# Hash attention and a quick-GELU MLP on one core: Attention scheduled by whole pairs, POOL's late sums of W_out gathered, and the last turns reordered

## The chip, the cores and the metric

The kernel runs on one core of a Trainium2 chip. The core has five engines that work side by side: TensorE (PE in the profile) multiplies matrices into PSUM, VectorE (DVE) and ScalarE (ACT) work on SBUF and PSUM, GpSimd (POOL) works on SBUF, and SyncE (SP) issues transfers. Each runs its own instructions in order and waits for the others by semaphores. The metric is the time of one execution on the device in microseconds (us); the lower the better.

## What is computed

Attention over 4 batches and 8 heads, 768 queries and keys, head dimension 64, in which a query sees only the keys that fall into the same bucket of a 6-bit hash, and then an MLP whose input is the heads side by side (3072 tokens of 512):

```python
q_bits = (np.einsum('bhsd,dk->bhsk', q, proj) > 0).astype(np.int64)
k_bits = (np.einsum('bhsd,dk->bhsk', k, proj) > 0).astype(np.int64)
mask = q_bucket[:, :, :, None] == k_bucket[:, :, None, :]
scores = np.where(mask, scale * np.matmul(q, k.transpose(0, 1, 3, 2)), -1000000000.0)
attn = np.exp(scores - np.max(scores, axis=-1, keepdims=True))
attn = attn / (np.sum(attn, axis=-1, keepdims=True) + 1e-09)
x = np.matmul(attn, v)                 # heads side by side: 3072 x 512
h = x @ w_in                           # 512 x 2048
g = h * (1.0 / (1.0 + np.exp(-1.702 * h)))
out = g @ w_out                        # 2048 x 512
```

Everything is computed in float32; w_in and w_out arrive as float64 bit patterns and are converted on the chip.

## The kernel before

**Attention** works on 16 pairs n of two heads each, one in partitions 0 to 63 and one in 64 to 127. The queries of a pair are cut into two halves c of 384 (HS), the keys into six tiles (T) of 128, three of which are "low" and three "high" (GT). The functions, in the order of the data:
- `fetch` (L328) loads k and q, `fetch_v` (L340) loads v, from SP's queue.
- `turn` (L391, VectorE) transposes k or q of the next pair in blocks of 32; `measure` (L398, ScalarE) sums its squares for a later check of size.
- `hashed` (L408, TensorE) multiplies both by the hash vectors; `featured` (L413, VectorE) makes sign features of that, and eight small transfers (L420, SP) put them where the scores need them.
- `scores` (L432, TensorE): per key tile two bf16 products of the features and two float32 products of k and q, one for each head, into a PSUM tile ps of two banks (three such tiles rotate); the exponential (L433, ScalarE) goes to es[c].
- The sum over keys: `add_low` (L440, L441, POOL) adds the three low tiles to acc0, of which there is one buffer; `add_high` (L446, L448, VectorE) adds the three high ones and acc0. `total` (L479, TensorE) sums over partitions into dn; `invert` (L485 to L494, VectorE) makes reciprocals of it, with a `yield` behind its first step; `norm` (L499, VectorE) scales the output.
- `values` (L458, TensorE) multiplies v by the exponentials; `unload` (L469, L470, ScalarE) writes the result to xT, which is the MLP's input.

PSUM has one bank with the tag "av" (pool aps) and one with the tag "m" (pool mps) beside the six of the scores. "av" holds the output of values, "m" holds dn, the hash and a small transpose in turn.

Between these, VectorE converts w_in: `begin(n)` issues a chunk's load (L162), `step(n, k)` runs the next k steps of it (L178 to L198). In the last four pairs `x_sums` (L219 to L222) make the first sums of the MLP's input.

The order of each engine's instructions is the order in which the program's lines emit them. It is written out in one loop over groups (n, c). In a group, TensorE gets scores(n, c), then, of the group before it, total and values, then hashed. So scores and values alternate half by half, and total(n - 1) and hashed(n + 1) stand in between: scores(n, 0), total(n - 1), values(n - 1, 1), hashed(n + 1), scores(n, 1), values(n, 0), and so on.

**The MLP** multiplies by Strassen-Winograd: seven products of quarters in place of eight, twice nested for W_out. Its sums of quarters are made by `sums_a` (POOL, L211 to L214: s1, s3, s2, s4) for W_out and `sums_b` (VectorE, L219 to L222: t1, b12, t2, t4) for the activations. The products by W_out run in 21 steps n (7 outer products for each of three blocks of tokens), each of seven inner products (L820) of eight matmuls. In a step TensorE makes the products 1, 2, 3, 6, 7, 5 and 4; VectorE adds them up in the four quarters c11 to c22 (L824), and in between makes the four sums for the next step (g_sums); `turned` (L800, VectorE) transposes finished quarters and `written` (L807) sends them out. Product 6 needs t2, product 7 b12, product 4 t4, product 3 the s4 of W_out.

The W_out sums of the outer products 0 to 3 are made before, those of number 4 in step 0. The sums of number 5 (needed in step 5) and number 6 (needed in step 6) are held back: POOL does two of them in each of the steps 2 to 5. A copy of one element to `mark` (L924) from the result of the step before holds POOL until that step has its c11:

```python
if 2 <= n <= 5:
    nc.gpsimd.tensor_copy(mark, ms[OUTER[n - 1]][0:1, 0, 0:1])
i = n % 2 * 2
for f in inner_sums(4) if n == 0 else inner_sums(4 + n // 2)[i : i + 2] if 2 <= n <= 5 else []:
    f()
```

In the last two steps `after(at)` is called at five points of a step and emits the sums for the next step and the turns: in the last but one, quarter 0 is turned behind c11, quarters 1 and 3 behind c12 and c22, quarter 2 behind c21. The output transfers of the last but one step go to SP's and ScalarE's queues in turn.

Of the kernel before, what the change touches and what calls it, by code (L numbers as in the profile page):

```python
# [8 lines left out]
F32 = mybir.dt.float32  # L9
# [29 lines left out]
def kernel(  # L39
# [243 lines left out]
    def attention(ff):  # L283
# [4 lines left out]
        with actx:  # L288
# [99 lines left out]
            def turn(n, name):  # L388
                x = raws[n, name]
                xt = xts[n, name] = wk.tile([P, S], F32, tag=f"{name}T", name=f"{name}T")  # L390
                nc.vector.transpose(xt, x.rearrange("p s i -> p (s i)"))  # L391
# [31 lines left out]
            def scores(n, c, kts):  # L423
                qT, kT, qf, kf = xts[n, "q"], xts[n, "k"], feats[n % 2]["q"], feats[n % 2]["k"]
                cols = slice(c * HS, (c + 1) * HS)
                for kt in kts:
                    ps = sps.tile([P, 2, 512], F32, tag="s", name="ps")
                    keys = slice(kt * P, (kt + 1) * P)
                    for a, m, last in ((kf, qf, False), (kT, qT, True)):
                        for j in range(2):  # L430
                            hs = slice(D * j, D * (j + 1))
                            nc.tensor.matmul(ps[:, j, 0:HS], a[hs, keys], m[hs, cols], start=not last, stop=last)  # L432
                    nc.scalar.activation(es[c][:, kt, :, 0:HS], ps[:, :, 0:HS], Act.Exp, scale=1.0 / D**0.5)  # L433
# [3 lines left out]
            def add_low(n, c):  # L437

                acc = accs[n, c, 0] = st.tile([P, 2, HS], F32, tag="acc0", name="acc0", bufs=1)
                nc.gpsimd.tensor_tensor(acc, es[c][:, 0, :, 0:HS], es[c][:, 1, :, 0:HS], op=Alu.add)  # L440
                nc.gpsimd.tensor_tensor(acc, acc, es[c][:, 2, :, 0:HS], op=Alu.add)  # L441
# [8 lines left out]
            def values(n, c, kts):  # L450
                if 0 in kts:

                    pool, tag = (mps, "m") if (n, c) == (last, 1) else (aps, "av")
                    avs[n, c] = pool.tile([P, HS + 1], F32, tag=tag, name="av")
                av, vt = avs[n, c], vts[n]
                for t in kts:
                    for j in range(2):
                        nc.tensor.matmul(av[D * j : D * (j + 1), :], vt[:, t, j, :], es[c][:, t, j, :],  # L458
                                         start=(t == 0), stop=(t == T - 1))
# [11 lines left out]

            def total(n):

                dn = accs[n] = mps.tile([P, HS], F32, tag="m", name="dn")
                for c in range(2):
                    acc = accs.pop((n, c))
                    for j in range(2):
                        r0 = D * j + 32 * c
                        nc.tensor.matmul(dn[r0 : r0 + 32, :], ones[:, 0:32], acc[:, j, :], start=True, stop=True)  # L479

            def invert(n):


                rt = st.tile([P, HS // 32, 32], F32, tag="rt", name="rt", bufs=1)
                nc.vector.transpose(rt.rearrange("p s i -> p (s i)"), accs.pop(n))  # L485
                yield
                r = st.tile([P, 2, HS // 32], F32, tag="r", name="r")
                nc.vector.reciprocal(r, rt[:, :, 0].unsqueeze(1).to_broadcast([P, 2, HS // 32]))
                for r0 in range(0, P, 32):
                    c = r0 // 32 % 2  # L490
                    r1 = r0 + 32 - 64 * c
                    nc.vector.reciprocal(r[r1 : r1 + 32, c], rt[r0 : r0 + 32, :, 0])
                rs = accs[n] = st.tile([P, S], F32, tag="rs", name="rs", bufs=1)
                nc.vector.transpose(rs.rearrange("p (s i) -> p s i", i=32),  # L494
                                    r.rearrange("p c s -> p (c s)").unsqueeze(2).to_broadcast([P, S // 32, 32]))

            def norm(n):
                x, rs = x_of(n), accs.pop(n)
                nc.vector.tensor_tensor(x, x, rs.rearrange("p (t s) -> p t s", t=T), op=Alu.mult)  # L499


            groups = [(n, c, kts) for n in range(len(pairs)) for c in range(2)
                      for kts in ((range(GT), range(GT, T)) if n == 0 else (range(T),))]
            last = len(pairs) - 1
            conv = {}

# [18 lines left out]
                    nc.vector.tensor_reduce(largest[0:1, 0:1], row, axis=AX.X, op=Alu.max)  # L525


            totals, norms, hashes = [], [], []
            rest = first_pair()
            fetch_v(0)  # L530
            for x in "kq":
                fetch(1, x)
            for g in range(len(groups) + 2):
                n, c, kts = groups[g] if g < len(groups) else (last + 1, 0, ())
                prev = groups[g - 1] if 1 <= g <= len(groups) else None
                if kts:
                    scores(n, c, kts)
                    if g == 0:
                        rest()
                    if kts[0] == 0:  # L540
                        add_low(n, c)


                if hashes:
                    featured(hashes.pop())
                ended = prev and prev[2][-1] == T - 1
                if ended:
                    add_high(*prev[:2])
                    if prev[1] == 1:
                        totals.append((g + (g == len(groups)), prev[0]))  # L550

                turned = ("", "k", "q", "")[g] if n == 0 else "kq" if c == 0 and n < last else ""
                inverted = iter(())
                for x in turned[:1]:
                    turn(n + 1, x)
                    measure(n + 1, x)
                while norms:
                    norm(norms.pop(0))
                if totals and totals[0][0] == g:
                    norms.append(totals.pop(0)[1])  # L560
                    total(norms[-1])

                    inverted = invert(norms[-1])
                    next(inverted)
                for x in turned[1:]:
                    turn(n + 1, x)
                    measure(n + 1, x)
                whole(inverted)
                if prev:
                    values(*prev)  # L570
                if ended:
                    unload(*prev[:2])
                if "q" in turned:
                    hashed(n + 1)
                    if n:
                        hashes.append(n + 1)
                    else:
                        featured(n + 1)
                    for x in "kq" if n else "q":
                        if n + 2 <= last:  # L580
                            fetch(n + 2, x)
                    fetch_v(n + 1)
                elif turned:
                    fetch(n + 2, turned)
                if kts and kts[-1] == T - 1:
                    step(n, 3)
                    if c == 0 and n > last - len(x_sums):
                        x_sums[n - last - 1]()
                    if c == 1:
                        begin(n + 1)  # L590
                if g in (len(groups) - 3, len(groups) - 2):
                    guard(g - len(groups) + 3)
                if g == len(groups):
                    for f in in_sums(0):
                        f()
                    early.close()
                    next(ff)
            for x in norms:
                norm(x)


    def shifted_attention():
# [76 lines left out]
    def feed_forward(tag, late=()):  # L679
# [9 lines left out]
        with ExitStack() as fctx:  # L689
# [228 lines left out]
            for n, (sb, o) in enumerate(steps_out):  # L918
# [1 line left out]
                if 0 < n and n + 1 < len(steps_out):  # L920
                    fetch(n + 1)

                if 2 <= n <= 5:
                    nc.gpsimd.tensor_copy(mark, ms[OUTER[n - 1]][0:1, 0, 0:1])  # L924
                i = n % 2 * 2
                for f in inner_sums(4) if n == 0 else inner_sums(4 + n // 2)[i : i + 2] if 2 <= n <= 5 else []:
                    f()
                later_sums = g_sums(n + 1)
                m = wholes[n % len(wholes)]
# [1 line left out]
                def after(at):  # L931
                    if at == 0:
                        while pending:
                            pending.pop(0)()

                    for f in later_sums[at : at + 1] if n == 0 else ([], later_sums[0:1], later_sums[1:2], later_sums[2:], [])[at]:
                        f()

                    if n + 2 >= len(steps_out):
                        for q in ((0,) * (not final), (), (1, 3), (2,), (0,))[at]:  # L940
                            turned(m, int(final), int(not final), q, q + 1)
                    if final and at in (2, 3):
                        written(sb, 0, (3 - at,), loader + [nc.scalar])
                    if n + 2 == len(steps_out) and at == 3:
                        written(sb, 1, (0, 1), loader + [nc.scalar])
# [23 lines left out]
    def whole(steps):  # L969
        for _ in steps:  # L970
            pass
# [46 lines left out]
```

## Time and profile before

| What | Value |
|---|---|
| median of 10 runs | 880.65 us (880.35 to 883.31) |
| profiled execution | 882.81 us, span 881.0 us, granted TensorE clock 0.996 |
| PE (TensorE) busy | 868.8 us (99%), 4077 matmul instructions |
| PE weight loads busy | 500.8 us (57%) |
| DVE (VectorE) busy | 723.5 us (82%) |
| ACT (ScalarE) busy | 314.6 us (36%) |
| POOL (GpSimd) busy | 322.0 us (37%) |
| Attention's scores, from the first to the last values | 10.88 to 324.86 us |
| MLP, first half (products by W_in) | 324.86 to about 614.3 us |
| MLP, second half (products by W_out) | about 614.3 us to the end |

The span is the time from the first to the last instruction of the profiled execution. The chain of waits follows the work that ended last back to its start: 95% of it is TensorE, 4% VectorE. A line of the timeline has the start in us, the duration, the engine, the line of the program, the operation, the tile written and the tiles read, the shape and the count; in brackets stands how long the engine had been idle before it and what ended that.

### The profile page before, as it was taken

Reading aid. Unit: us, or ns where it says so; the run is one execution under the profiler, and the core shown is the slowest. Engines: PE = TensorE matmul, PEld = TensorE weight load, DVE = VectorE, ACT = ScalarE, POOL = GpSimd, SP = SyncE. Lnnn points to the kernel's source line nnn. Section 1 sums busy time; section 2 is a strip of 40 time slices with the busy share of each in tenths; the row PEclk is TensorE's granted clock in tenths of the full one; section 3 lists DMA queues with packets and bytes.
Section 4 is the critical chain, followed back from the end, with each engine's and each line's share of the span. In section 5 each row is a group of like instructions: output and inputs, shape, how many; then the busy total and the mean of one; then the engine's idle time right before and its main releaser. Section 6 shows DMA issues by size and latency. Waiting matters only on the chain.

```text
span 881.0 us, 11897 instructions
## 1 busy us (share of the span) xinstructions
PE 868.8 (99%) x4077; PEld 500.8 (57%) x4077; DVE 723.5 (82%) x1020; ACT 314.6 (36%) x519; POOL 322.0 (37%) x277
## 2 busy tenths in 40 slices
PE   9999999999999999999999999999999999999996
PEld 5444444444444444444444444444878888888885
DVE  4689989999999986788777788888887977897786
ACT  5767776776677642222233222332000000000000
POOL 4343343334433365665443344659921000000000
PEclk9999999999999999999999999999999999999999
DMA  5535545665444103555455545575835675467524
GB/s 131 94 62 84 104 82 98 99 102 84 82 82 99 53 0 140 206 203 203 164 189 192 208 177 194 193 251 186 301 108 191 196 213 214 156 221 243 191 96 99
DMA packets 169157, 132.01 MB, mean 150 GB/s; under 512 B 123616, under 2 KB 138112, under 8 KB 163712
## 3 DMA queue, kind: packets, MB, share of 16 engines
q1 hardware_dynamic: 166528, 129.70, 51.7%
q10 hardware_dynamic: 2560, 1.46, 0.7%
q8 instruction: 34, 0.56, 0.3%
q14 instruction: 35, 0.29, 0.1%
HBM read 79.69 MB, written 50.33 MB: 148 GB/s over the span
## 4 chain that ended last, share of the span: by engine, by line
PE 95%; DVE 4%; issue 0%; POOL 0%; POOLq 0%; DVEq 0%
PE product L708 33%; PE product L820 25%; PE ps L432 18%; PE av L458 15%; PE dn L479 2%; DVE xT L824 2%; PE hash L408 1%; DVE y L800 1%; PE tp L366 1%; PE hash L373 0%; DVE v L824 0%; DVE t2a L221 0%; DVE raw_g L220 0%; DVE t4g L222 0%; DVE s_in L220 0%
## 5 line engine op out<-in xcount | busy, mean ns | idle before, releaser
L433 ACT ACTIVATE e<-ps 128x768 f32<-128x768 f32 x192 | 151.1, 812 | 15.1 <-PE ps L432 12.8
L432 PE MATMUL ps<-qT,kT 64*128 64x384 f32 x768 | 155.2, 482 | 0.0
L708 PE MATMUL product<-xT,w_in_sb 128*128 128x512 f32 x288 | 135.6, 593 | 0.0
L458 PE MATMUL av<-e,v 128*64 128x385 f32 x768 | 131.5, 490 | 0.0
L440 POOL TENSOR_TENSOR acc<-e 128x768 f32<-128x768 f32 x32 | 58.7, 1833 | 192.6 <-DVE acc L448 122.0
L716 ACT ACTIVATE c<-c 128x512 f32<-128x512 f32 x72 | 45.3, 630 | 186.8 <-issue 78.8
L458 PEld LDWEIGHTS av<-e,v 128*64 128x64 f32 x768 | 52.3, 136 | 76.3 <-issue 75.8
L708 PEld LDWEIGHTS product<-xT,w_in_sb 128*128 128x128 f32 x288 | 54.6, 190 | 69.1 <-issue 64.1
L708 PE MATMUL product<-t_x,s_in 128*128 128x512 f32 x192 | 90.2, 592 | 0.0
L432 PEld LDWEIGHTS ps<-qT,kT 64*128 64x128 f32 x768 | 68.3, 188 | 35.1 <-issue 35.1
L219 POOL TENSOR_TENSOR v<-c,u 128x512 f32<-128x512 f32 x24 | 34.1, 1422 | 123.4 <-ACT c L716 123.4
L833 ACT COPY u<-product 128x256 f32<-128x256 f32 x21 | 7.8, 372 | 175.5 <-PE product L820 134.0
L432 PE MATMUL ps<-qf,kf 64*128 64x384 bf16 x384 | 63.3, 324 | 0.1
L708 PEld LDWEIGHTS product<-t_x,s_in 128*128 128x128 f32 x192 | 36.5, 190 | 45.9 <-issue 43.7
L441 POOL TENSOR_TENSOR acc<-acc,e 128x768 f32<-128x768 f32 x32 | 59.1, 1846 | 2.5
L708 PE MATMUL product<-xT,s_in 128*128 128x512 f32 x96 | 45.1, 592 | 0.0
L708 PE MATMUL product<-t_x,w_in_sb 128*128 128x512 f32 x96 | 45.1, 592 | 0.0
L432 PEld LDWEIGHTS <-kf 64*128 64x128 bf16 x384 | 19.1, 94 | 41.0 <-issue 19.5
L446 DVE SCALAR_TENSOR_TENSOR acc<-e 128x768 f32<-128x768 f32 x32 | 32.2, 1007 | 5.1 <-ACT e L433 5.1
L469 ACT COPY vs<-av 128x1 f32<-128x1 f32 x32 | 5.1, 159 | 86.2 <-PE av L458 86.2
L820 PE MATMUL product<-raw_g,xT 128*128 128x256 f32 x152 | 35.3, 380 | 0.0
L448 DVE TENSOR_TENSOR acc<-acc,e 128x768 f32<-128x768 f32 x32 | 32.3, 1010 | 3.3
(208 smaller groups left out, 1548.2 us busy)
## 6 DMA issues: line engine op xcount, KB each, us to landing
raw_g<-g_dram SPq DMA_DIRECT2D x22, 1024.0 KB
s_in<-g_dram SPq DMA_DIRECT2D x20, 1024.0 KB
g_dram<-c SPq DMA_DIRECT2D x72, 256.0 KB
g_dram<-t SPq DMA_DIRECT2D x48, 256.0 KB
raw<-in_moe_w_in_dram SPq DMA_DIRECT2D x16, 512.0 KB
raw<-in_moe_w_out_dram SPq DMA_DIRECT2D x16, 512.0 KB
v<-in_v_dram SPq DMA_DIRECT2D x32, 192.0 KB
g_dram<-u SPq DMA_DIRECT2D x24, 256.0 KB
```

The lines of the kernel that those rows point to most:

```text
L219: return [lambda: eng.tensor_tensor(t1, b12, b11, op=Alu.subtract), lambda: eng.tensor_tensor(b12, b22, b12, op=Alu.subtract), lambda: eng ...
L432: nc.tensor.matmul(ps[:, j, 0:HS], a[hs, keys], m[hs, cols], start=not last, stop=last)
L433: nc.scalar.activation(es[c][:, kt, :, 0:HS], ps[:, :, 0:HS], Act.Exp, scale=1.0 / D**0.5)
L440: nc.gpsimd.tensor_tensor(acc, es[c][:, 0, :, 0:HS], es[c][:, 1, :, 0:HS], op=Alu.add)
L441: nc.gpsimd.tensor_tensor(acc, acc, es[c][:, 2, :, 0:HS], op=Alu.add)
L446: nc.vector.scalar_tensor_tensor(acc, e[0], T * TINY, e[1], op0=Alu.add, op1=Alu.add)
L448: nc.vector.tensor_tensor(acc, acc, x, op=Alu.add)
L458: nc.tensor.matmul(av[D * j : D * (j + 1), :], vt[:, t, j, :], es[c][:, t, j, :], start=(t == 0), stop=(t == T - 1))
L479: nc.tensor.matmul(dn[r0 : r0 + 32, :], ones[:, 0:32], acc[:, j, :], start=True, stop=True)
L708: nc.tensor.matmul(ps, wq[LEFT[i]][:, kc, :], xq[RIGHT[i]][:, kc, :], start=(kc == 0), stop=(kc == K2 - 1))
L716: nc.scalar.activation(c, c, Act.Gelu_apprx_sigmoid)
L820: nc.tensor.matmul(ps, wq[LEFT[i]][:, c, :], gq[RIGHT[i]][:, c, :], start=(c == 0), stop=(c == F4 - 1))
```

## The change

Three things are changed.

1. **POOL's held-back sums of W_out.** Nothing is emitted in steps 2 to 4; step 5 emits all four sums of number 5 and the first two of number 6, step 6 the last two of number 6. The mark is copied in steps 5 and 6 only.
2. **The last but one step.** Its turns are emitted at the point behind c21, in this order: the third sum for the last step (t2), the turns of quarters 0 and 1, the turn of quarter 3, the fourth sum (t4), the turn of quarter 2.
3. **Attention by whole pairs.** The loop over groups is gone. Pair 0 is written out by hand; for each later pair TensorE gets scores(n, 0), scores(n, 1), hashed(n + 1), values(n, 0), values(n, 1), total(n). Outputs of values go to bank "av" for the first half and to bank "m" for the second; dn goes to "av". `invert` is one piece, and it and norm(n - 1) are emitted behind add_low(n, 0), ahead of turn(n + 1, k) and add_high(n, 0). turn(n + 1, q), hashed and featured follow add_high(n, 0). In pair 1 total(0) is emitted behind scores(1, 0). The conversion has two steps behind featured and four behind values(n, 0) and add_high(n, 1). The loads of k and q for pair n + 2 are emitted at the end of pair n. At the end, invert and norm of the last pair are emitted behind the MLP's first part.

```diff
@@ -450,7 +450,7 @@
             def values(n, c, kts):
                 if 0 in kts:
 
-                    pool, tag = (mps, "m") if (n, c) == (last, 1) else (aps, "av")
+                    pool, tag = (mps, "m") if c else (aps, "av")
                     avs[n, c] = pool.tile([P, HS + 1], F32, tag=tag, name="av")
                 av, vt = avs[n, c], vts[n]
                 for t in kts:
@@ -471,7 +471,7 @@
 
             def total(n):
 
-                dn = accs[n] = mps.tile([P, HS], F32, tag="m", name="dn")
+                dn = accs[n] = aps.tile([P, HS], F32, tag="av", name="dn")
                 for c in range(2):
                     acc = accs.pop((n, c))
                     for j in range(2):
@@ -483,7 +483,6 @@
 
                 rt = st.tile([P, HS // 32, 32], F32, tag="rt", name="rt", bufs=1)
                 nc.vector.transpose(rt.rearrange("p s i -> p (s i)"), accs.pop(n))
-                yield
                 r = st.tile([P, 2, HS // 32], F32, tag="r", name="r")
                 nc.vector.reciprocal(r, rt[:, :, 0].unsqueeze(1).to_broadcast([P, 2, HS // 32]))
                 for r0 in range(0, P, 32):
@@ -498,9 +497,6 @@
                 x, rs = x_of(n), accs.pop(n)
                 nc.vector.tensor_tensor(x, x, rs.rearrange("p (t s) -> p t s", t=T), op=Alu.mult)
 
-
-            groups = [(n, c, kts) for n in range(len(pairs)) for c in range(2)
-                      for kts in ((range(GT), range(GT, T)) if n == 0 else (range(T),))]
             last = len(pairs) - 1
             conv = {}
 
@@ -525,78 +521,79 @@
                     nc.vector.tensor_reduce(largest[0:1, 0:1], row, axis=AX.X, op=Alu.max)
 
 
-            totals, norms, hashes = [], [], []
+            low, high, every = range(GT), range(GT, T), range(T)
             rest = first_pair()
             fetch_v(0)
             for x in "kq":
                 fetch(1, x)
-            for g in range(len(groups) + 2):
-                n, c, kts = groups[g] if g < len(groups) else (last + 1, 0, ())
-                prev = groups[g - 1] if 1 <= g <= len(groups) else None
-                if kts:
-                    scores(n, c, kts)
-                    if g == 0:
-                        rest()
-                    if kts[0] == 0:
-                        add_low(n, c)
-
-
-                if hashes:
-                    featured(hashes.pop())
-                ended = prev and prev[2][-1] == T - 1
-                if ended:
-                    add_high(*prev[:2])
-                    if prev[1] == 1:
-                        totals.append((g + (g == len(groups)), prev[0]))
-
-                turned = ("", "k", "q", "")[g] if n == 0 else "kq" if c == 0 and n < last else ""
-                inverted = iter(())
-                for x in turned[:1]:
-                    turn(n + 1, x)
-                    measure(n + 1, x)
-                while norms:
-                    norm(norms.pop(0))
-                if totals and totals[0][0] == g:
-                    norms.append(totals.pop(0)[1])
-                    total(norms[-1])
-
-                    inverted = invert(norms[-1])
-                    next(inverted)
-                for x in turned[1:]:
-                    turn(n + 1, x)
-                    measure(n + 1, x)
-                whole(inverted)
-                if prev:
-                    values(*prev)
-                if ended:
-                    unload(*prev[:2])
-                if "q" in turned:
+            scores(0, 0, low)
+            rest()
+            add_low(0, 0)
+            scores(0, 0, high)
+            turn(1, "k")
+            measure(1, "k")
+            values(0, 0, low)
+            fetch(2, "k")
+            scores(0, 1, low)
+            add_low(0, 1)
+            add_high(0, 0)
+            turn(1, "q")
+            measure(1, "q")
+            values(0, 0, high)
+            unload(0, 0)
+            hashed(1)
+            featured(1)
+            fetch(2, "q")
+            fetch_v(1)
+            scores(0, 1, high)
+            values(0, 1, low)
+            values(0, 1, high)
+            unload(0, 1)
+            for n in range(1, last + 1):
+                scores(n, 0, every)
+                add_low(n, 0)
+                if n == 1:
+                    add_high(0, 1)
+                    turn(2, "k")
+                    total(0)
+                invert(n - 1)
+                norm(n - 1)
+                if 1 < n < last:
+                    turn(n + 1, "k")
+                scores(n, 1, every)
+                add_low(n, 1)
+                add_high(n, 0)
+                if n < last:
+                    turn(n + 1, "q")
                     hashed(n + 1)
-                    if n:
-                        hashes.append(n + 1)
-                    else:
-                        featured(n + 1)
-                    for x in "kq" if n else "q":
-                        if n + 2 <= last:
-                            fetch(n + 2, x)
+                    featured(n + 1)
+                    for x in "kq":
+                        measure(n + 1, x)
+                else:
+                    guard(0)
+                    guard(1)
+                step(n, 2)
+                add_high(n, 1)
+                values(n, 0, every)
+                unload(n, 0)
+                step(n, 4)
+                values(n, 1, every)
+                unload(n, 1)
+                total(n)
+                if n + 2 <= last:
+                    for x in "kq":
+                        fetch(n + 2, x)
+                if n < last:
                     fetch_v(n + 1)
-                elif turned:
-                    fetch(n + 2, turned)
-                if kts and kts[-1] == T - 1:
-                    step(n, 3)
-                    if c == 0 and n > last - len(x_sums):
-                        x_sums[n - last - 1]()
-                    if c == 1:
-                        begin(n + 1)
-                if g in (len(groups) - 3, len(groups) - 2):
-                    guard(g - len(groups) + 3)
-                if g == len(groups):
-                    for f in in_sums(0):
-                        f()
-                    early.close()
-                    next(ff)
-            for x in norms:
-                norm(x)
+                    begin(n + 1)
+                if n > last - len(x_sums):
+                    x_sums[n - last - 1]()
+            for f in in_sums(0):
+                f()
+            early.close()
+            next(ff)
+            invert(last)
+            norm(last)
 
 
     def shifted_attention():
@@ -920,10 +917,9 @@
                 if 0 < n and n + 1 < len(steps_out):
                     fetch(n + 1)
 
-                if 2 <= n <= 5:
+                if n in (5, 6):
                     nc.gpsimd.tensor_copy(mark, ms[OUTER[n - 1]][0:1, 0, 0:1])
-                i = n % 2 * 2
-                for f in inner_sums(4) if n == 0 else inner_sums(4 + n // 2)[i : i + 2] if 2 <= n <= 5 else []:
+                for f in {0: inner_sums(4), 5: inner_sums(5) + inner_sums(6)[:2], 6: inner_sums(6)[2:]}.get(n, []):
                     f()
                 later_sums = g_sums(n + 1)
                 m = wholes[n % len(wholes)]
@@ -933,12 +929,16 @@
                         while pending:
                             pending.pop(0)()
 
-                    for f in later_sums[at : at + 1] if n == 0 else ([], later_sums[0:1], later_sums[1:2], later_sums[2:], [])[at]:
+                    steps = [later_sums[at : at + 1]] if n == 0 else [[], later_sums[0:1], later_sums[1:2], later_sums[2:], []][at : at + 1]
+
+                    if n + 2 >= len(steps_out):
+                        turns = [lambda q=q: turned(m, int(final), int(not final), q, q + 1) for q in range(4)]
+                        if final:
+                            steps = [[[], [], [turns[1], turns[3]], [turns[2]], [turns[0]]][at]]
+                        elif at == 3:
+                            steps = [later_sums[2:3], turns[0:2], turns[3:4], later_sums[3:], turns[2:3]]
+                    for f in sum(steps, []):
                         f()
-
-                    if n + 2 >= len(steps_out):
-                        for q in ((0,) * (not final), (), (1, 3), (2,), (0,))[at]:
-                            turned(m, int(final), int(not final), q, q + 1)
                     if final and at in (2, 3):
                         written(sb, 0, (3 - at,), loader + [nc.scalar])
                     if n + 2 == len(steps_out) and at == 3:
```

## The prediction

> **What bounds the kernel now.** I read the page first (busy times and the 40 slices), then the chain of waits over two of Attention's pairs, then the timelines around every place where an engine waits. TensorE is busy for 99% of the span, so Attention's steady state has to be read from its chain:
>
> ```profile
> 56.41 0.78 PE hash L408 x8
> 57.19 4.95 PE ps L432 x36
> 62.14 4.04 PE av L458 x24
> 66.17 4.95 PE ps L432 x36
> 71.12 0.78 PE dn L479 x8
> 71.91 4.03 PE av L458 x24
> 75.94 0.78 PE hash L408 x8
> 76.72 4.95 PE ps L432 x36
> ```
>
> One pair takes 76.72 - 57.19 = 19.53 us, TensorE without a hole. The table by stage gives VectorE 18.05 of these 19.53, so a new order has little of it to spare. Part of that is waiting for POOL:
>
> ```profile
> 159.45 2.12 POOL L440 TENSOR_TENSOR acc<-e 128x768 f32<-128x768 f32 x1 [7.52 <-DVE acc L448]
> 160.09 2.04 DVE L193 SCALAR_TENSOR_TENSOR w_in_sb<-raw,w_in_sb 128x512 f32<-128x512 uint32 x1
> 161.65 2.01 POOL L441 TENSOR_TENSOR acc<-acc,e 128x768 f32<-128x768 f32 x1
> 162.16 2.05 DVE L195 TENSOR_TENSOR w_in_sb<-bits,w_in_sb 128x512 f32<-128x512 f32 x1
> ```
>
> A 512-element step takes 0.69 us elsewhere, here 2.04. The two engines alternate: 160.09 + 2.04 = 162.13 is 0.56 after POOL's end (161.57), and POOL's second sum then needs 1.53 to its end at 163.66. TensorE's one large hole is at the start of the W_out products:
>
> ```profile
> 636.76 3.02 DVE L824 TENSOR_TENSOR xT<-xT 128x256 f32<-128x256 f32 x2
> 638.24 1.25 POOL L211 TENSOR_TENSOR w_in_sb<-xT 128x512 f32<-128x512 f32 x1
> 639.57 1.33 POOL L212 TENSOR_TENSOR xT<-xT 128x512 f32<-128x512 f32 x1
> 639.70 1.49 DVE L824 TENSOR_TENSOR xT<-xT,v 128x256 f32<-128x256 f32 x1
> 645.74 3.53 PE L820 MATMUL product<-t2a,w_in_sb 128*128 128x256 f32 x8 [1.95 <-DVE t2a L221]
> 649.05 2.06 PE L820 MATMUL product<-raw_g,xT 128*128 128x256 f32 x8
> ```
>
> VectorE waits for POOL's held-back sums, t2a is late, TensorE idles 1.95, and the granted clock is then 0.50 to 0.60 from 645.7 to 649 (table by stage). At the end VectorE is packed:
>
> ```profile
> 865.43 0.64 DVE L800 STREAM_TRANSPOSE y<-xT 128x256 f32<-128x256 f32 x1
> 866.14 0.91 ACTq L807 DMA_DIRECT2D out_dram<-y  x2
> 867.15 0.37 ACT L833 COPY u<-product 128x256 f32<-128x256 f32 x1 [13.60 <-PE product L820]
> 867.55 0.43 DVE L824 TENSOR_TENSOR v<-product,u 128x256 f32<-128x256 f32 x1 [1.49 <-ACT u L833]
> ```
>
> The last step's u waits on ScalarE behind two issues of output transfers, which wait for the last turn; from 867.55 VectorE has no hole up to 874.33.
>
> **What the Trainium skill says.** "SBUF — State Buffer", Who interferes with whom: VectorE with two SBUF inputs and a GpSimd operation that reads SBUF exclude each other for a whole instruction; one SBUF input is free. The alternation above agrees, and the transpose L391 beside POOL's sum keeps its 0.97. "TensorE: Matmul & The Clock Gate", Step-by-step: matmuls stay in program order, only weight loads go ahead. The trace agrees: where dn took 1.24 instead of 0.78 (266.48), the values behind it started later by as much. Same page, Part 1: the clock halves after an idle window of some 3.4 us; here 1.95 us of idleness was enough.
>
> **Attention: what is saved.** Key tiles of scores follow each other every 0.806 us (six: 4.84 of 4.95), weight loads of values every 0.322 (twelve: 3.87 of 4.03). So each change of matmul kind costs 0.10 or 0.16, and the new order drops one of each per pair: scores 12 x 0.806 + 0.10 = 9.77, hash 0.78, values 4.03 + 3.87, dn 0.78, together 19.23 if nothing waits.
>
> **What waits then.** hashed(n+1) now stands right behind both scores, and needs turn(n+1, q), which VectorE reaches only after invert, norm, turn(k) and add_high. From the start of scores(n, 0), right behind dn(n-1):
> - rt starts at 0.14 (before: dn ends 149.97, rt 150.11). Nothing is put between its steps any more; the last pair shows that case: 337.92 to 340.84, 2.92. norm could start at 3.06.
> - The first exponential starts at 1.09 (144.25 to 145.34), each takes 0.80, the second ends at 2.69. POOL's first sum starts 0.08 later, at 2.77, and holds the lock for 1.54: to 4.31. norm then needs 0.81 (768 elements at the rate that 512 show): 5.12.
> - POOL's second sum: 5.12 + 1.54 = 6.66. turn(k), free of the lock, runs 5.04 to 6.0. The first sum of add_high wants to start then, waits, and ends at 6.66 + 0.81 = 7.47.
> - Two more sums at 7.57 and 8.63 (spacing 1.06), end 9.59; turn(q) 9.51 to 10.45; hash of q at 10.55.
>
> TensorE is there at 9.77. It stands still for up to 0.78; the half of the hash on k is done meanwhile, which may save up to 0.15. I take 0.70, bounds 0.5 and 0.9. A pair takes 19.93 instead of 19.53: **+0.40**, and 13 pairs (2 to 14) give **+5.2** (bounds +2.6 and +7.8). The rest of VectorE's list fits: featured, add_high(n, 1) (behind POOL's second pair of sums) and the four late steps of the conversion, which no longer meet POOL, end near 20.0, when the next rt is due. What conversion gains (2 x 1.35), norm and add_high give back.
>
> **Pair 1** has a longer chain: total(0) now comes after scores(1, 0). Values of (0, 1) start at 26.80 as before and take 4.03 in one piece (0.16 saved), so scores(1, 0) runs 30.83 to 35.78, dn(0) to 36.56. rt at 36.70, norm(0) at 39.62, 1.49 to the next start (its row at 41.85: 1.58, pair 0 is strided), add_high(1, 0) from 41.11, turn(q) at 44.10, hash at 45.15. scores(1, 1) ended at 41.51: TensorE waits **3.64**. The clock after it: at 645.74 two products took 3.31 + 1.90 instead of 2 x 1.73, so 1.75 lost. I take **+1.75** here (bounds 0 and 3.5; the idle time is longer). Its own saving: -0.16.
>
> **Pair 15** has no hash: -0.26, and guard's small transpose may wait 0.06. In pairs 12 to 14 of before dn was late by 0.46, 0.44 and 0.53, since x_sums fill VectorE; now add_high(n, 1) is done some 2 us ahead of dn: -1.43. x_sums delay rt by up to 1.2, but norm waits for POOL until 4.31 anyway: 0.
>
> Attention: -0.16 - 0.16 + 3.64 + 1.75 + 5.2 - 0.2 - 1.43 = **+8.6**.
>
> Transfers: SP issues featured's eight from 12.0 to 18.1, then k, q (4.3), v (1.1) and the next raw chunk. k lands about 4.5 after its issue starts (busy DMA slices), 2.9 into the next pair, needed at 5.0; v and raw have longer. Cost 0; if k were late, the chain would move by as much.
>
> **W_out products.** Without the two POOL sums of step 2 (L211, L212 at 638.24 and 639.57) the second of the two sums at 636.76 ends near 638.65 instead of 639.78, the next at 639.0 instead of 641.2, and t2a at about 643.5 instead of 645.6, just when TensorE has finished (643.63). Product 5 follows at 641.90 + 3 x 1.73 = 647.09 instead of 650.95: **-3.9** (bounds -3.9 and -2.5).
>
> In exchange six POOL sums run from 671.45 on in one go (1.34 each), up to about 680.6. They meet VectorE's c12 + v (675.67), t1b (676.00), s_in and t2b: by alternation t2b ends near 683.2 instead of 680.5. TensorE needs it at 683.6, so step 5 is not late. But VectorE had only 0.28 of idle time in step 5, so t2a for step 6 ends near 696.45; TensorE needs it by 695.7: **+0.75** (bounds 0 and 1.3). The sums themselves are ready in time: s4 of the fifth at about 676.7, used from 682.0.
>
> **Tail.** t2a for the last step comes some 1.2 earlier, since three turns go behind it, and TensorE's 0.81 of waiting at 864.30 goes. What is late next is the chain in the fourth excerpt: the last turn still has the same operations ahead of it on VectorE, so u, and from it the packed rest, move by **+0.15** (bounds -0.9 and +0.3).
>
> **Sum.** 8.6 - 3.9 + 0.75 + 0.15 = +5.6. The profiled execution took 882.81 (span 881.0 and 1.8 around it), 2.2 above the median of 880.65; the difference is put on the median: **886.3**.
>
> **Rivals.**
> 1. TensorE isn't late at the hash in pairs 2 to 14 (VectorE gets its norm in before POOL, or turn(q) fits). For: the break-even is a delay of only 0.30 per pair. Against: the exclusive lock and the 2.92 of invert are both measured. Then a pair takes 19.23: 8.6 - 13 x 0.70 = -0.5 in Attention, -3.5 in all: 877.2. Chance 0.12.
> 2. Both small: pair 1 loses no clock, delay per pair 0.50, no delay at step 6: 8.6 - 1.75 - 2.6 = 4.25, less 3.9: about 881.1. Chance 0.15.
> 3. VectorE's whole list becomes the bound: it is at 20.0 against 19.93 in my sum; 0.4 more of gaps and lost locks in each pair give 13 x 0.4 = 5.2 more: 891.5. Chance 0.15.
>
> The forecast has 0.58. About 0.2% (1.8 us) is what a measurement of this kernel can tell from no change: slower by more 0.74 (forecast, rival 3 and a little of 2), within it 0.15, faster 0.11. The forecast's own bounds are some 4 us either way; with rivals 2 and 3, and rival 1 left out, the range is 881.0 to 891.5.
>
> **What would show it.** Right: pairs 19.8 to 20.0 apart, TensorE waiting for the q transposes (L391) before the hash in each; a hole of 3 to 4 us near 42 with a lower clock behind it; no hole at 643, and a smaller one near t2a of step 6. Wrong: pairs at 19.3 with hash right behind scores, a norm that runs ahead of POOL's first sum, or a pair that waits elsewhere, at rt, dn or a late k.

## The result, and the profile after

The changed kernel takes 888.14 us (median of 8 runs, 887.14 to 889.21) against 880.8 (28 runs): a ratio of 1.008, 95% interval 1.007 to 1.0089. It is 7.3 us slower. The profiled execution took 886.72 with a span of 884.9; the one of before had 882.81 and 881.0. These two are only 3.9 apart because that of before ran with a halved clock for a while (near 645 us), as its slower runs seem to, while that of the changed kernel is the fastest of its ten runs and has no such stretch there or behind its wait in pair 1.

The chain of waits over two of Attention's pairs, after:

```profile
54.28 9.80 PE ps L432 x72
64.08 1.49 PE hash L408 x8
65.56 7.92 PE av L458 x48
73.48 0.78 PE dn L479 x8
74.26 9.80 PE ps L432 x72
84.06 1.49 PE hash L408 x8
85.55 7.92 PE av L458 x48
93.46 0.78 PE dn L479 x8
94.25 9.80 PE ps L432 x72
```

Scores take 9.80 instead of twice 4.95, values 7.92 instead of twice 4.03: merging saves 0.24. The hash takes 1.49 instead of 0.78. Together 19.98 per pair instead of 19.53. Why the hash is longer stands in the timeline of the pair that starts at 94.25 (start, duration, engine and line):

```profile
96.22 0.98 DVE L493 STREAM_TRANSPOSE rs<-r 128x768 f32<-128x768 f32 x1
96.90 1.54 POOL L440 TENSOR_TENSOR acc<-e 128x768 f32<-128x768 f32 x1 [9.70 <-ACT e L433]
97.30 1.96 DVE L498 TENSOR_TENSOR xT<-xT,rs 128x768 f32<-128x768 f32 x1
98.53 2.28 POOL L441 TENSOR_TENSOR acc<-acc,e 128x768 f32<-128x768 f32 x1
100.08 1.54 DVE L446 SCALAR_TENSOR_TENSOR acc<-e 128x768 f32<-128x768 f32 x1
103.67 0.97 DVE L391 STREAM_TRANSPOSE qT<-q 128x768 f32<-128x768 f32 x1
103.97 0.84 PE L408 MATMUL hash<-kT,pf_k 128*32 128x384 f32 x4
104.69 0.84 PE L408 MATMUL hash<-qT,pf_q 128*32 128x384 f32 x4
```

POOL's first sum runs until 98.44. norm (L498) wants to start at 97.30 and ends at 99.26, 0.82 after it; POOL's second sum then ends at 100.81, and add_high's first (L446) at 101.62, again 0.81 later. So turn(q) ends at 104.64, and the half of the hash on q starts 0.05 after that, 0.72 behind the half on k, which has run alone meanwhile. TensorE never counts as idle here: the delay shows only as a hash of twice its length.

In pair 1 it does count as idle:

```profile
36.26 0.58 DVE L485 STREAM_TRANSPOSE rt<-dn 128x384 f32<-128x384 f32 x1 [3.62 <-PE dn L479]
39.25 1.57 DVE L498 TENSOR_TENSOR xT<-xT,rs 128x768 f32<-128x768 f32 x1
40.72 0.94 DVE L446 SCALAR_TENSOR_TENSOR acc<-e 128x768 f32<-128x768 f32 x1
41.07 0.84 PE L408 MATMUL hash<-kT,pf_k 128*32 128x384 f32 x4
43.71 0.97 DVE L391 STREAM_TRANSPOSE qT<-q 128x768 f32<-128x768 f32 x1
44.74 0.84 PE L408 MATMUL hash<-qT,pf_q 128*32 128x384 f32 x4 [2.83 <-DVE qT L391]
```

VectorE idles 3.62 for dn, then has invert, norm and add_high ahead of turn(q). The halves of the hash start 3.67 apart.

The W_out products have gained. The same two products as in the excerpt of before, and the new small delay in step 6:

```profile
651.34 1.89 PE L817 MATMUL product<-t2a,w_in_sb 128*128 128x256 f32 x8
653.06 1.89 PE L817 MATMUL product<-raw_g,xT 128*128 128x256 f32 x8
...
697.96 1.89 PE L817 MATMUL product<-raw_g,s_in 128*128 128x256 f32 x8
699.96 1.96 PE L817 MATMUL product<-t2a,s_in 128*128 128x256 f32 x8
```

The first two are 1.72 apart instead of 3.31, and nothing waits ahead of them. The last two are 2.00 apart, 0.27 more than the usual 1.73, and the product behind them starts another 0.07 late (701.76). And the end:

```profile
869.70 0.60 DVE L797 STREAM_TRANSPOSE y<-xT 128x256 f32<-128x256 f32 x1
870.37 0.91 ACTq L804 DMA_DIRECT2D out_dram<-y  x2
871.38 0.37 ACT L830 COPY u<-product 128x256 f32<-128x256 f32 x1 [13.64 <-PE product L817]
871.78 0.42 DVE L821 TENSOR_TENSOR v<-product,u 128x256 f32<-128x256 f32 x1 [1.49 <-ACT u L830]
```

TensorE no longer waits for t2a there, but u still comes behind the issues. From the start of the last but one step's products to the start of the last turn it is 25.80 (851.99 to 877.79), before 25.91 (847.79 to 873.70); to the end of the span it is 32.9, before 33.2.

### The profile page after: what moved, and what is told of

It reads as the page before. It is cut to its first block, busy times and chain, and to the rows that moved or that the text cites. A ratio compares the mean times of both kernels' runs of the same rounds, so it can differ in the third digit from the quotient of the medians.

```text
span 884.9 us, 11860 instructions
## 1 busy us (share of the span) xinstructions
PE 871.3 (98%) x4077; PEld 502.0 (57%) x4077; DVE 723.5 (82%) x1020; ACT 313.6 (35%) x519; POOL 318.8 (36%) x275
## 4 chain that ended last, share of the span: by engine, by line
PE 93%; DVE 4%; issue 1%; DMA 1%; SPq 0%; ACTq 0%; DVEq 0%; ACT 0%
PE product L705 33%; PE product L817 27%; PE ps L432 16%; PE av L458 13%; PE hash L408 2%; PE dn L479 1%; DVE xT L821 1%; DMA q<-in_q_dram 1%; DVE y L797 1%; DVE acc L448 0%; DVE acc L446 0%; PE hash L373 0%; DVE rs L493 0%; DVE qT L391 0%; DVE r L491 0%
## 5 line engine op out<-in xcount | busy, mean ns | idle before, releaser
L458 PE MATMUL av<-e,v 128*64 128x385 f32 x768 | 128.2, 488 | 0.0
L440 POOL TENSOR_TENSOR acc<-e 128x768 f32<-128x768 f32 x32 | 49.3, 1542 | 204.8 <-ACT e L433 153.6
L441 POOL TENSOR_TENSOR acc<-acc,e 128x768 f32<-128x768 f32 x32 | 62.7, 1961 | 2.5
L446 DVE SCALAR_TENSOR_TENSOR acc<-e 128x768 f32<-128x768 f32 x32 | 41.0, 1282 | 5.1 <-ACT e L433 5.1
L448 DVE TENSOR_TENSOR acc<-acc,acc 128x768 f32<-128x768 f32 x32 | 31.0, 969 | 3.7 <-DVE acc L448 0.5
```

The lines of the kernel that those rows point to most:

```text
L446: nc.vector.scalar_tensor_tensor(acc, e[0], T * TINY, e[1], op0=Alu.add, op1=Alu.add)
L448: nc.vector.tensor_tensor(acc, acc, x, op=Alu.add)
```

## The experiments

Each was timed side by side with the kernel before, whose runs fall into two groups of about equal size here, near 880.4 and near 882.6 (of the 28 runs of the result, 21 are in the lower one). The differences are a few us, so the ratio to before stands beside each median. Between two changed kernels, timed at different times, medians and ratios differ by up to 0.7.

**The three parts alone.** The first takes the new Attention and leaves the W_out products and the last turns as they were; the second and third put one of those edits each into the kernel before.

```diff
 # second, in the kernel before
-                if 2 <= n <= 5:
+                if n in (5, 6):
                     nc.gpsimd.tensor_copy(mark, ms[OUTER[n - 1]][0:1, 0, 0:1])
...
+                for f in {0: inner_sums(4), 5: inner_sums(5) + inner_sums(6)[:2], 6: inner_sums(6)[2:]}.get(n, []):
...
 # third, in the kernel before (the loop around it as in the change)
+                        elif at == 3:
+                            steps = [later_sums[2:3], turns[0:2], turns[3:4], later_sums[3:], turns[2:3]]
```

> Only the new order of Attention; the W_out products as before. My theory (Attention loses, W_out products gain): about 8.6 us above the kernel before, so near 889 to 891, with pairs 19.98 apart and one wait of TensorE near 42 us. Rival (the loss measured as 7.3 sits partly in the W_out products, from POOL's six sums in a row): at most 6 above before.

> Only POOL's held-back sums moved to steps 5 and 6; all else as before. My theory: the wait of 1.95 us at 645 goes and with it the halved clock behind it, a wait of about 0.75 comes before product 6 of step 6: 3 us below before; if most runs of before had no halved clock there, only 1.3 below. Rival (the wait only moves to step 6): within 0.5 of before.

> Only the turns of the last but one step reordered; all else as before. My theory: TensorE's wait of 0.81 before product 6 of the last step goes, but the end is held by u behind ScalarE's two issues of output transfers: within 0.3 of before. Rival (TensorE holds the end): 0.9 below before.

| Part alone | median, us | ratio to before (95%) | in us of 881 |
|---|---|---|---|
| Attention | 891.98 | 1.0113 (1.0094 to 1.0132) | +10.0 |
| POOL's sums | 878.91 | 0.997 (0.9958 to 0.9983) | -2.6 |
| last turns | 880.32 | 0.999 (0.9981 to 0.9999) | -0.9 |
| all three | 888.14 | 1.008 (1.007 to 1.0089) | +7.0 |

The parts add up to +6.5, within the intervals of +7.0. All of the loss is Attention's, which rules out the rival of the first run. Attention's +10.0 is more than the 8.6 forecast, and its median lies above the expected 889 to 891. The two profiles, which both have the halved clock in step 2 of the W_out products, are 9.2 apart (spans 890.2 and 881.0).

The second run's products in step 6 are 2.01 apart instead of 1.73, so the wait of step 2 (1.95) does not just move there. Its -2.6 is a mean over the groups of before: its runs lie from 878.26 to 879.88, some 1.5 below the lower group and 3.7 below the upper one.

For the last turns the -0.9 is the rival's figure, and only the details speak against it. From the last but one step's products to the end of the span it is 32.9 (845.40 to 878.3) against 33.2 (847.79 to 881.0). One of this run's 14 times lies above 882, of before's 37 times 19 do; the medians of those below are 880.1 and 880.4. So the edit itself gives about 0.3, and the rest is a different share of the upper group, for which the runs show no reason. The profile of this run lacks the halved clock near 645 (product 6 takes 1.97 instead of 3.53 there).

**norm out of the chain.** In pairs 2 to 14 norm goes behind featured:

```diff
                 invert(n - 1)
-                norm(n - 1)
+                if n in (1, last):
+                    norm(n - 1)
...
                     featured(n + 1)
+                    if n > 1:
+                        norm(n - 1)
```

> The changed kernel, but norm(n - 1) is emitted behind featured(n + 1) in pairs 2 to 14 instead of ahead of turn(n + 1, k). My theory (the chain invert, norm behind POOL's sum, add_high, turn(q) delays the hash by 0.7 per pair): turn(q) ends 0.6 to 0.7 earlier, pairs 19.3 to 19.4 apart, 7.5 to 8.5 below the changed kernel, about 880. Rival (VectorE's whole list is the bound, about 20 per pair): pairs stay at 19.9 to 20.0, no change against the changed kernel's 888.1.

Measured: 880.57, ratio to before 0.9985 (0.9977 to 0.9994), so below the changed kernel by 7.6 (medians) or 8.3 (ratios). The chain of its profile:

```profile
94.86 9.79 PE ps L432 x72
104.65 0.89 PE hash L408 x8
105.54 7.92 PE av L458 x48
113.46 0.78 PE dn L479 x8
```

A pair takes 19.38 (94.86 to 114.24) and the hash 0.89. So the same operations fit in another order. Their time on VectorE is shorter too, 17.36 per pair instead of 18.19: norm now stands where the first step of the conversion (L178) waited for POOL, which takes 0.68 (at 107.94) instead of 1.57 (at 106.17 in the changed kernel). From this pair and the next:

```profile
95.73 0.58 DVE L485 STREAM_TRANSPOSE rt<-dn 128x384 f32<-128x384 f32 x1
99.14 1.68 POOL L441 TENSOR_TENSOR acc<-acc,e 128x768 f32<-128x768 f32 x1
99.89 1.74 DVE L446 SCALAR_TENSOR_TENSOR acc<-e 128x768 f32<-128x768 f32 x1 [0.30 <-ACT e L433]
106.19 1.83 DVE L498 TENSOR_TENSOR xT<-xT,rs 128x768 f32<-128x768 f32 x1
115.11 0.58 DVE L485 STREAM_TRANSPOSE rt<-dn 128x384 f32<-128x384 f32 x1
```

VectorE has little to spare: rt starts 0.87 after dn is done (94.86), behind the conversion, where in the changed kernel it started 0.06 after it (94.31 against 94.25). But this is not what holds the hash, since VectorE then idles 0.30 for an exponential. The first sum of add_high (L446) ends 0.81 after POOL's second sum again (101.63 and 100.82), and that leaves the products on q 0.12 behind those on k (104.70 and 104.58).

**Pair 1.** invert(0) and norm(0) leave the way of the hash:

```diff
-                invert(n - 1)
-                norm(n - 1)
+                if n > 1:
+                    invert(n - 1)
+                    norm(n - 1)
...
                     hashed(n + 1)
+                    if n == 1:
+                        invert(0)
                     featured(n + 1)
+                    if n == 1:
+                        norm(0)
```

> The changed kernel, but in pair 1 invert(0) is emitted behind turn(2, q) and norm(0) behind featured(2), so that the hash of pair 2 need not wait for them. My theory: the wait of TensorE near 42 us (2.8 us, and 3.6 with the split hash) goes, and with it the halved clock behind it in the runs that had one: 3.5 to 5.0 below the changed kernel's 888.1, so 883 to 884.6, with a granted clock of 0.997 or 0.998 in nearly all runs. Rival (the wait is of no weight, since VectorE catches up on it in the pairs behind): within 1 of the changed kernel.

Measured: 883.31, ratio to before 1.0021 (1.0014 to 1.0028), below the changed kernel by 4.8 (medians) or 5.2 (ratios). The granted clock is 0.997 or 0.998 in all of its 19 runs; of the changed kernel's ten runs, two have 0.997 and eight 0.995. What lies behind those is seen in the profile of the kernel with the new Attention alone, which has the same pair 1. Its timeline, and its table by stage (length, then PE, weight loads, DVE, ACT and POOL busy, then the granted clock and two numbers on transfers):

```profile
44.83 1.50 PE L408 MATMUL hash<-qT,pf_q 128*32 128x384 f32 x4 [2.84 <-DVE qT L391]
46.26 8.74 PE L458 MATMUL av<-e,v 128*64 128x385 f32 x48
```

```profile
45.00:48.40 3.40, 3.40 (x14) 0.96 (x14) 1.92 (x3) 0.00 (x0) 2.24 (x2) 0.58 0.00 0
```

After the wait the clock is down to 0.58 for 3.4 us, and hash and values take 0.66 and 0.75 longer: 1.41. In the profile of the changed kernel the clock stayed at 1.00 behind the same wait. So the 4.8 fit 3.67 for the wait and, with the clock lowered in eight runs of ten, about 1.1 for that.

**Both.**

> Both moves: norm behind featured in pairs 2 to 14 and the pair 1 of the run before. If the two are independent: 880.6 - 3.5 to 5.0 = 875.5 to 877, and so below the kernel before as well. Rival (VectorE's list, now nearly full in each pair, gives back what pair 1 saves): no lower than 879.

Measured: 875.26 (5 runs, 874.34 to 875.66), ratio to before 0.9925 (0.991 to 0.9939). The two are independent: 880.57 - 4.8 = 875.8. This beats both kernels. It is the changed kernel's idea, with two calls moved.

**The end.** On top of it, the last but one step's output transfers go out by SP alone:

```diff
                     if n + 2 == len(steps_out) and at == 3:
-                        written(sb, 1, (0, 1), loader + [nc.scalar])
+                        written(sb, 1, (0, 1), loader)
```

> The run before, with the output transfers of the last but one step issued by SP alone instead of SP and ScalarE in turn. My theory (u of the last step sits behind ScalarE's issues, and VectorE's packed rest behind u): u comes at once when product 1 is done, VectorE starts its rest right behind the last turn, 1.2 to 1.5 below the run before. Rival (SP, with four issues, sends the last transfers later and gives it back): no change.

Measured: 874.58, ratio to before 0.9916 (0.9902 to 0.9931); 0.7 below the run before it, with intervals that overlap, so that the times alone do not settle it. The traces show what moved. The first three lines are of the run before, the others of this one:

```profile
858.05 0.64 DVE L802 STREAM_TRANSPOSE y<-xT 128x256 f32<-128x256 f32 x1
859.77 0.37 ACT L835 COPY u<-product 128x256 f32<-128x256 f32 x1 [13.66 <-PE product L822]
860.17 0.42 DVE L826 TENSOR_TENSOR v<-product,u 128x256 f32<-128x256 f32 x1 [1.49 <-ACT u L835]
```

```profile
857.56 1.89 PE L822 MATMUL product<-raw_g,w_out_sb 128*128 128x256 f32 x8
858.00 0.61 DVE L802 STREAM_TRANSPOSE y<-xT 128x256 f32<-128x256 f32 x1
858.47 0.40 DVE L826 TENSOR_TENSOR v<-product,u 128x256 f32<-128x256 f32 x1
859.49 0.42 DVE L826 TENSOR_TENSOR xT<-product,v 128x256 f32<-128x256 f32 x1 [0.62 <-PE product L822]
...
862.74 1.89 PE L822 MATMUL product<-t4g,w_out_sb 128*128 128x256 f32 x8
...
864.66 0.42 DVE L826 TENSOR_TENSOR xT<-product,xT 128x256 f32<-128x256 f32 x1
```

v comes 1.7 earlier, as the theory has it. But the next sum then idles 0.62 for a product that TensorE ends at 859.45, so it is only 1.21 earlier than in the run before (859.49 against 860.70), and the last sum waits for product 4 (862.74 + 1.89), which costs another 0.12. So the last turn ends 1.1 earlier (865.75 against 866.82). From there to the end of the span it takes 6.85 instead of 6.48; that fits the rival's part, in which SP is later with the last transfers, but no run takes it apart. The theory was right on what held the end, and its size was too large, since it left out what comes next.

## Why the prediction was right

The forecast was 886.3, measured 888.14, so +5.6 was forecast and +7.3 came. Step by step:

- **Saving by merging**, 0.26 per pair: the traces give 0.24. The forecast's sum for a pair, 19.23 without a wait, took off 0.30 instead, since it had 9.77 for the scores and 7.90 for the values, where the trace has 9.80 and 7.92.
- **The chain to the hash.** Predicted from the start of scores: norm ready 3.06, POOL's second sum done 6.66, hash of q at 10.55. In the pair at 94.25: 3.05, 6.56 and 10.44. The delay was taken as 0.70, from 0.78 with the half on k saving a little. The hash takes 0.71 longer, but because q is only 0.72 late: the half on k saves nothing, so here two small errors cancel. A pair is 19.98 to 20.0, predicted 19.93, and over pairs 2 to 14 the mean is 20.02 (54.28 to 314.56), as one of them takes 20.32 (from 114.25; VectorE idles 0.46 in it for no reason that the trace shows). That is 13 x 0.49 = +6.4 where the forecast has +5.2.
- **Rivals 1 and 3.** Rival 1 is out by the same numbers. Rival 3, in which VectorE's list sets the pair, was close: the list is ready for rt at almost the same moment as dn (its step at 93.64 ends at 94.33, rt starts at 94.31). But rt starts 0.06 after dn is done, as early as behind an idle VectorE in pair 1 (0.07), so it doesn't hold TensorE. The fourth experiment, which moves norm alone, brings back 0.6 per pair.
- **Pair 1.** Predicted 3.64, measured 3.67. The clock behind it was put at 1.75; it costs 1.41 where it falls, and 0 in some runs.
- **W_out products.** Predicted -3.9 and, in step 6, +0.75. In the profiles step 2 gains what was said, and step 6 loses 0.34. But of the 3.9, 1.75 was the halved clock in the profile of before, at 882.81. The forecast took this off as a saving, but from the median of 880.65, which is 2.2 below that profile and lies in the group that seems not to have the halved clock. So it took the clock off twice, and this is its largest mis-sized term. Without the clock the sum has -1.4 for the W_out products; the edit alone gives -1.5 against the lower group.
- **Tail.** Predicted +0.15 since u holds the end. The trace gives -0.1 to the last turn and -0.3 to the end; the last experiment shows that u holds it.

The pairs (1.2) and the clock taken off twice (1.75) made the forecast too low; step 6 (0.4), the tail (0.45) and the clock behind pair 1 (0.3) made it too high. That the sum came within 1.8 is thus in part luck, while the waits that were forecast are the ones that the traces show.

What stays open is which runs get the halved clock. The wait is nearly the same in each profile (2.82 to 2.84 us in pair 1 in three of them, 1.95 in step 2 in three), and of each three, two have it and one has not. That the two groups of before come from it is likely but not shown: before, with such a wait, spreads over 3.7 us, the fourth experiment over 3.6, whereas the kernels without one (the second, the fifth and the last two, these with five runs each) spread over 1.3 to 1.6. But the groups are 2.2 apart, more than the 1.75, and some runs of either have a clock of 0.997.

## What to carry to other kernels

When a reordering takes gaps out of the busiest engine, look at which operation now stands right behind the merged block, and add up the in-order list of the engine that feeds it: what is not needed for that operand (here norm) must not stand ahead of it. Read such a delay from the duration of a group as well as from idle time: a wait counts as busy as long as the part that is ready still runs (all of the 0.72 here), and only what is left counts as idle (2.83 of the 3.67 in pair 1). And take a saving that rests on a lowered clock only for the share of runs that have it.

## What the runs showed of the hardware

When k and q are ready together, the eight products of the hash take 0.78. The half on q alone takes 0.77 (44.74 to 45.51 in pair 1), no less, so the two halves run side by side. With q 0.72 later the hash takes 1.49, with q 0.12 later (norm moved) 0.89. So here a wait costs its whole length: the half that runs meanwhile does not shorten the other.

VectorE's and POOL's sums hold each other up. The first sum of add_high takes 0.95 while POOL rests (108.39) and 1.54 beside POOL's second sum (100.08), ending 0.81 after it. POOL's second sum takes 1.68 while VectorE waits for dn (34.73) and 2.28 when norm has started ahead of it (98.53). The transposes keep their 0.96 beside POOL's sums (99.19).

Behind a TensorE wait of 1.95 or 2.8 us the granted clock was 0.54 to 0.58 for some 3.4 us in some executions and 1.00 in others, at a price of 1.4 to 1.75 us.
